# Attention's loads issued as pairs of half-size transfers, in a fused mLSTM, MoE and MLP kernel

## The chip, the cores and the metric

The kernel runs on one core of a Trainium2 chip. The metric is device time in microseconds (us): of the kernel before, three runs gave 765.03 (median), 762.16 and 768.67. One further execution was profiled; the rows below are all of that execution.

## The reference, cut to what matters

Three stages follow each other. The first is a gated linear attention with a running state (mLSTM) over 4 batches, 8 heads, 768 steps and head dimension 40:

```python
for t in range(S):
    m_new = np.maximum(f_gate[:, :, t] + m, i_gate[:, :, t])
    f_stab = np.exp(f_gate[:, :, t] + m - m_new)
    i_stab = np.exp(i_gate[:, :, t] - m_new)
    C = f_stab[:, :, None, None] * C + i_stab[:, :, None, None] * np.einsum('bhd,bhe->bhde', vt, kt)
    n = f_stab[:, :, None] * n + i_stab[:, :, None] * kt
    ...
    y[:, :, t] = o * h_tilde / denom
```

The second sends each of the 3072 tokens to one of 8 experts of 384 places each (a greedy assignment by sorted logits) and computes `relu(x @ w1[e]) @ w2[e]`, with 320, 1024 and 320 features. The third is a dense `elu(x @ w_in) @ w_out` with 320, 2048 and 320 features. Only attention's loads are touched by the change.

## The kernel before, in words

**Attention** takes the sequence in 12 chunks of 64 steps and the batches in 2 pairs, which makes 24 units; `Attention.run` works through one unit u in each turn of its loop. Partitions 0 to 63 of a tile belong to one batch of the pair, 64 to 127 to the other. A unit needs two loads from HBM:

- `qk`: `self.QK[u]`, a tile of 128 partitions x (2, 8, 64) f32, keys first and queries second. The first four units load all 128 partitions (512 KB), later ones the 80 that hold data (320 KB). There are four such tiles, used in turn.
- `vk`: `self.VK[u]`, 128 partitions x 968 f32 (values, keys by token and output gates; 484 KB). There are six buffers.

In a turn, TensorE does the scores of unit u+2 (`scores`, L302) mixed with the products of unit u+1's queries with the state (`recall`, L391), then `P` times values (`values`, L377) mixed with the state's update (`state`, L404), then transposes and router logits (L446, L460) and the decay matrix of unit u+2 (`decay`, L311 to L315), which ScalarE turns into `W` (L317). VectorE weighs the scores (L356), adds the states (L415) and finishes the unit's rows `x` (L424 to L429), which GpSimd scales (L430).

**Weight chunks.** Beside attention, the MLP's weights are brought in and converted, a chunk `cx` at a time: `pull` issues the load of a chunk at the end of a turn (through `fetch`, L914), and `win_pieces` converts it on ScalarE (`cg`, L926, and `cF`, L933), VectorE (L939, L942) and GpSimd. There are 15 chunks: eight of `w_in` in 128 partitions (512 KB), two of `w_in` that are already brought in as two loads of 64 partitions (`lo` and `up`, 256 KB each, rows of 1 KB), and five of `w_out` (448 KB). Three buffers hold them.

**Order.** All these loads, and the stores of the finished rows (`rows_out`, L439: two of 64 partitions, 80 KB each), are issued by SyncE, strictly in program order; a load that must wait holds up all that stand behind it. `tie` makes the load of `vk` for unit u+4 wait for an operation of VectorE in turn u (`seeded`, L367), and that of `qk` for unit u+5 for another (`summed`, L415). Each transfer that SyncE issues takes one of eight semaphores in turn (DMAHW0 to DMAHW7 in the order's rows) and waits until the transfer that had it before has landed: eight can be under way.

After attention comes the router, then `Mlp.run`, a planned sequence over eight rounds of one expert each and the dense MLP on the same rows.

Of the kernel before, what the change touches and what calls it, by code (L numbers as in the profile page):

```python
# [119 lines left out]
class Attention:  # L120
# [150 lines left out]
    def load_qk(self, u, other=None):  # L271
        self.QK[u] = self.QKb[u % 4]
        z = slice(0, 128) if u < 4 else slice(64 - D, 64 + D)
        self.tie(self.nc.sync.dma_start(self.QK[u][z], self.qk[u, z]), other)

    def load_vk(self, u, other=None):
        self.VK[u] = self.two.tile([128, 968], F32, name="vk", bufs=6)
        self.tie(self.nc.sync.dma_start(self.VK[u], self.vk[u]), other)

    def value(self, u, h, r):  # L280
        return self.VK[u][r:r + 64, h * 41:h * 41 + 64]
# [596 lines left out]
class Mlp:  # L878
# [76 lines left out]
    def win_pieces(self, stage):  # L955

        nc = self.nc
        A, G = nc.scalar, nc.gpsimd
        wide = self.win.dtype != F32
        n = 512  # L960
        al, lo, up = slice(0, 128), slice(0, 64), slice(64, 128)
        tiles = {}
        total = 10 + EARLY * 320 // 448
        self.piece = self.got = 0

        def whole():
            return stage.tile([128, n], F32, name="cF")

        def get(i):
            k, h = divmod(i, 4)  # L970
            cs = slice(h * n, h * n + n)
            tiles[i] = [stage.tile([128, n, 2], I32, name="cx", bufs=3) if wide else None, None, None if wide else whole()]
            if i >= 10:
                cs = slice((i - 10) * 448, (i - 10) * 448 + 448)
                tiles[i] = [t if t is None else t[:, :448] for t in tiles[i]]
                loads = [(al, self.src(self.wout, al, cs))]
            elif k < 2:
                loads = [(al, self.src(self.win, slice(k * 128, k * 128 + 128), cs))]
            else:
                w = self.src(self.win, slice(256, 320), slice(h * 1024, h * 1024 + 1024))  # L980
                w = w.rearrange("p (k e t) -> e p k t", k=4, e=2)
                loads = [(lo, w[0]), (up, w[1])]
            self.fetch(loads, wide, tiles[i])

        def pull():
            if self.got < min(total, self.piece + 2 + wide):
                get(self.got)
                self.got += 1

        self.pull = pull  # L990
        for i in range(total):
            self.piece = i
            while i not in tiles:
                yield
            k, h = divmod(i, 4)
            cs = slice((i - 10) * 448, (i - 10) * 448 + 448) if i >= 10 else slice(h * n, h * n + n)
            if wide:
                w = 448 if i >= 10 else n
                tiles[i][1:] = stage.tile([128, n], F32, name="cg")[:, :w], whole()[:, :w]
            F = tiles[i][2]  # L1000
            yield from self.conv(wide, tiles.pop(i), top=True)
            if i >= 10:
                A.activation(self.first[0][:, cs], F, AF.Copy)
                yield
                nc.vector.tensor_tensor(self.first[1][:, cs], F, self.first[0][:, cs], op=ALU.subtract)
            elif k < 2:
                A.activation(self.wih[:, k, cs], F, AF.Copy)
                yield
                G.tensor_tensor(self.wil[:, k, cs], F, self.wih[:, k, cs], op=ALU.subtract)
            else:  # L1010
                w = self.wis.rearrange("p (k e t) -> p k e t", e=2, t=128)[:, 4 * h:4 * h + 4]
                F = F.rearrange("p (k t) -> p k t", t=128)
                A.activation(w[lo, :, 0], F[lo], AF.Copy)
                yield
                A.activation(w[up, :, 1], F[up], AF.Copy)
                yield
                nc.vector.tensor_tensor(w[up, :, 0], F[lo], w[lo, :, 0], op=ALU.subtract)
                yield
                nc.vector.tensor_tensor(w[lo, :, 1], F[up], w[up, :, 1], op=ALU.subtract)
            yield  # L1020
# [588 lines left out]
```

## Time and profile before

| | |
|---|---|
| median of three runs | 765.03 us |
| profiled execution | 764.96 us |
| its span, first to last instruction | 763.2 us |
| what lies outside the span | 1.76 us |
| TensorE busy in the span | 92% |
| mean granted TensorE clock | 0.96 of full speed |
| all loads and stores of SyncE's queue (q1) | 35.12 MB, 15.3% of the 16 DMA engines' span |

The profile's busy times are sums over the whole program, in which stages with different limits follow each other; a change in attention is read from the stretch of attention alone (0 to some 150 us). "DMA share" is the busy share of the 16 DMA engines; it can be a little over 1, since packets overlap. "Issue" in a list of waits or in the chain is time in which an engine waited for nothing that the profile shows.

### The profile page before, as it was taken

How to read it: one execution, taken by the hardware profiler on the slowest of the kernel's cores; microseconds unless marked ns; L12 is line 12 of the kernel's file. 1: busy time of each engine (PE TensorE's matmuls, PEld its weight loads, DVE VectorE, ACT ScalarE, POOL GpSimd, SP SyncE). 2: the span in 40 equal slices, each digit the busy share in tenths (PEclk: the TensorE clock that was granted, in tenths of full speed). 3: DMA queues.
4: the chain of work that ended last, by engine and by line, in shares of the span. 5: the costliest groups of instructions: out<-in, count | busy, mean ns of one | idle time of the engine just before them, and what ended most of it. 6: DMA issues, size and time to landing. Idle time of an engine off the chain costs nothing.

```text
span 763.2 us, 17860 instructions
## 1 busy us (share of the span) xinstructions
PE 702.8 (92%) x7229; PEld 639.9 (84%) x7232; DVE 545.0 (71%) x1610; ACT 377.9 (50%) x804; POOL 185.1 (24%) x242
## 2 busy tenths in 40 slices
PE   7788888825999999999999999999999999999994
PEld 4556566613989999998999999999999999999994
DVE  7786988876888968975796698569768824841551
ACT  4654445424465725742782366257527734642542
POOL 5564744225311401310211120112032310001001
PEclk9898999955999999999999999999999999999998
DMA  8686968236101400500220230023013321100000
GB/s 303 184 267 188 257 211 246 56 97 205 38 1 49 148 9 9 170 18 10 94 85 27 84 95 2 27 84 96 1 61 107 95 79 34 35 1 27 1 1 26
DMA packets 22435, 67.29 MB, mean 88 GB/s; under 512 B 3536, under 2 KB 7632, under 8 KB 22352
## 3 DMA queue, kind: packets, MB, share of 16 engines
q1 hardware_dynamic: 14240, 35.12, 15.3%
q0 software_dynamic: 8064, 30.94, 12.4%
q8 instruction: 56, 0.92, 0.5%
q14 instruction: 27, 0.22, 0.1%
q10 hardware_dynamic: 48, 0.10, 0.0%
HBM read 58.28 MB, written 7.86 MB: 87 GB/s over the span
## 4 chain that ended last, share of the span: by engine, by line
PE 74%; issue 11%; DVE 9%; ACT 2%; POOL 1%; DMA 1%; POOLq 0%; DVEq 0%; ACTq 0%
PE ph L1184 31%; PE acc L1323 6%; PE acc L1327 6%; PE acc L1324 6%; PE acc L1291 3%; PE pO L377 3%; PE acc L1293 2%; PE acc L1292 2%; PE pR L391 2%; PE pX L460 2%; PE acc L1278 1%; PE pX L446 1%; PE acc L1280 1%; PE pS L302 1%; PE ph L1137 1%
## 5 line engine op out<-in xcount | busy, mean ns | idle before, releaser
L1237 DVE SCALAR_TENSOR_TENSOR e<-e,ph 128x384 f32<-128x384 f32 x128 | 70.4, 551 | 51.5 <-ACT e L1234 50.8
L1233 ACT ACTIVATE e<-ph 128x384 f32<-128x384 f32 x128 | 62.3, 487 | 80.7 <-PE ph L1184 75.8
L1184 PE MATMUL ph<-yh,wih 128*128 128x384 f32 x256 | 89.5, 349 | 0.7 <-DVE xl L1145 0.3
L1201 ACT ACTIVATE gh<-ph 128x384 fp32r<-128x384 f32 x64 | 31.4, 491 | 115.4 <-PE ph L1184 87.0
L1184 PE MATMUL ph<-yh,wil 128*128 128x384 f32 x256 | 86.6, 338 | 0.0
L1333 POOL DMA_INDIRECT out_dram<-ot,idx x24 | 24.0, 1001 | 219.1 <-ACT ot L1054 216.2
L1061 DVE TENSOR_TENSOR gl<-e,gh 128x384 fp32r<-128x384 f32 x128 | 71.1, 562 | 1.8 <-ACT gh L1054 0.4
L1234 ACT ACTIVATE e<-e 128x384 f32<-128x384 f32 x128 | 67.3, 526 | 4.2
L1323 PE MATMUL acc<-woh,gh 128*128 128x320 f32 x216 | 68.3, 316 | 0.0
L1208 DVE SCALAR_TENSOR_TENSOR gl<-ph,gh 128x384 fp32r<-128x384 f32 x64 | 35.3, 553 | 45.6 <-ACT gh L1201 45.5
L1327 PE MATMUL acc<-woh,gl 128*128 128x320 f32 x216 | 66.8, 309 | 0.5 <-DVE gl L1061 0.5
L1324 PE MATMUL acc<-wol,gh 128*128 128x320 f32 x216 | 66.7, 309 | 0.0
L1184 PE MATMUL ph<-yl,wih 128*128 128x384 f32 x256 | 66.5, 341 | 0.0
L1054 ACT ACTIVATE gh<-e 128x384 fp32r<-128x384 f32 x96 | 49.0, 514 | 11.5 <-DVE e L1237 11.2
L1327 PE MATMUL acc<-woa,gl 128*128 128x320 f32 x168 | 52.4, 312 | 0.8 <-DVE gl L1061 0.8
L1323 PE MATMUL acc<-woa,gh 128*128 128x320 f32 x168 | 53.1, 316 | 0.0
L1184 PEld LDWEIGHTS ph<-yh,wih 128*128 128x128 f32 x256 | 48.2, 188 | 4.7 <-ACT yh L1296 4.1
L1324 PE MATMUL acc<-wob,gh 128*128 128x320 f32 x168 | 51.9, 309 | 0.0
L1184 PEld LDWEIGHTS ph<-yh,wil 128*128 128x128 f32 x256 | 48.1, 188 | 0.0
L1184 PEld LDWEIGHTS ph<-yl,wih 128*128 128x128 f32 x256 | 46.2, 188 | 0.0
L1065 POOL DMA_INDIRECT stg<-in_w1a_dram,wi x16 | 15.8, 985 | 122.5 <-DVE wi L819 117.3
L1184 PE MATMUL ph<-yh,wis 128*128 128x384 f32 x128 | 44.8, 350 | 0.0
(282 smaller groups left out, 2039.0 us busy)
## 6 DMA issues: line engine op xcount, KB each, us to landing
vk<-in_vk_dram SPq DMA_DIRECT2D x24, 484.0 KB, 5.6
qk<-in_qk_dram SPq DMA_DIRECT2D x20, 320.0 KB, 4.8
cx<-in_win_dram SPq DMA_DIRECT2D x8, 512.0 KB, 4.5
xd<-x SPq DMA_DIRECT2D x48, 80.0 KB, 3.1
wx<-in_wout_dram SPq DMA_DIRECT2D x9, 320.0 KB, 3.0
cx<-in_wout_dram SPq DMA_DIRECT2D x5, 448.0 KB, 4.2
qk<-in_qk_dram SPq DMA_DIRECT2D x4, 512.0 KB, 6.4
cx<-in_win_dram SPq DMA_DIRECT2D x4, 256.0 KB, 6.7
```

Source lines behind the costliest of these rows:

```text
L1054: self.nc.scalar.activation(out, x, AF.Copy)
L1061: self.nc.vector.tensor_tensor(out, x, y, op=ALU.subtract)
L1184: PE.matmul(p, w, x, start=k == 0, stop=k == 7)
L1201: nc.scalar.activation(h, p, AF.Relu)
L1208: nc.vector.scalar_tensor_tensor(l, p, 0.0, h, op0=ALU.max, op1=ALU.subtract)
L1233: nc.scalar.activation(e, p, AF.Relu, scale=-1.0)
L1234: nc.scalar.activation(e, e, AF.Exp, scale=-1.0)
L1237: nc.vector.scalar_tensor_tensor(e, e, -1.0, p, op0=ALU.add, op1=ALU.max)
L1323: PE.matmul(p, h[:, c], wh, start=f == 0, stop=False)
L1324: PE.matmul(p, h[:, c], wl, start=False, stop=False)
L1327: PE.matmul(p, l[:, c], wh, start=False, stop=f == 15)
L1333: s = nc.gpsimd.indirect_dma_start(out=self.out, out_offset=bass.IndirectOffsetOnAxis(ap=idx[:, t:t + 1], axis=0), in_=o, in_offset=None)
```

## The change

Three groups of loads are each issued as two transfers of half the bytes, into the same tiles. `qk` is divided between keys and queries (each half still has all its partitions, with rows of 2 KB instead of 4 KB), `vk` and the `cx` chunks of 128 partitions into partitions 0 to 63 and 64 to 127. Both halves of a load are tied to the same operation. The two chunks that were already divided, the stores, and everything after attention stay as they are.

```diff
     def load_qk(self, u, other=None):
         self.QK[u] = self.QKb[u % 4]
         z = slice(0, 128) if u < 4 else slice(64 - D, 64 + D)
-        self.tie(self.nc.sync.dma_start(self.QK[u][z], self.qk[u, z]), other)
+        for k in range(2):
+            self.tie(self.nc.sync.dma_start(self.QK[u][z, k], self.qk[u, z, k]), other)
 
     def load_vk(self, u, other=None):
         self.VK[u] = self.two.tile([128, 968], F32, name="vk", bufs=6)
-        self.tie(self.nc.sync.dma_start(self.VK[u], self.vk[u]), other)
+        for r in (0, 64):
+            self.tie(self.nc.sync.dma_start(self.VK[u][r:r + 64], self.vk[u, r:r + 64]), other)
...
             if i >= 10:
                 cs = slice((i - 10) * 448, (i - 10) * 448 + 448)
                 tiles[i] = [t if t is None else t[:, :448] for t in tiles[i]]
-                loads = [(al, self.src(self.wout, al, cs))]
+                loads = [(p, self.src(self.wout, p, cs)) for p in (lo, up)]
             elif k < 2:
-                loads = [(al, self.src(self.win, slice(k * 128, k * 128 + 128), cs))]
+                loads = [(slice(r, r + 64), self.src(self.win, slice(k * 128 + r, k * 128 + r + 64), cs)) for r in (0, 64)]
```

The order of SyncE's queue in the middle of attention, before: one turn's loads and stores, and what each waits for (a row's first name is the tile written).

```order
L439 DMA xd<-x 64x320 [waits DMAHW5_49,Pool_49]
L439 DMA xd<-x 64x320 [waits DMAHW6_49]
L914 DMA cx<-in_win_dram 128x1024 [waits DMAHW7_49,Activation_49]
L278 DMA vk<-in_vk_dram 128x968 [waits DMAHW0_49,DVE_49]
L274 DMA qk_112<-in_qk_dram 80x1024 [waits DMAHW1_49,DVE_49]
```

The same place in the changed kernel (its lines after the edits lie one or two lower):

```order
L441 DMA xd<-x 64x320 [waits DMAHW1_49,Pool_49]
L441 DMA xd<-x 64x320 [waits DMAHW2_49]
L916 DMA cx<-in_win_dram 64x1024 [waits DMAHW3_49,Activation_49]
L916 DMA cx<-in_win_dram 64x1024 [waits DMAHW4_49]
L280 DMA vk<-in_vk_dram 64x968 [waits DMAHW5_49,DVE_49]
L280 DMA vk<-in_vk_dram 64x968 [waits DMAHW6_49]
L275 DMA qk_112<-in_qk_dram 80x512 [waits DMAHW7_49,DVE_49]
L275 DMA qk_112<-in_qk_dram 80x512 [waits DMAHW0_49,PE_49]
```

Nothing changes places; a turn issues eight transfers instead of five, so the eight semaphores come round within one turn. Before, the first load that had to wait for a semaphore was the small `wg` (L160), the eighth of SyncE's queue; now it is a half of unit 1's `vk`.

On ScalarE the first consumers of the loads, before:

```order
L351 ACTIVATE sg<-vk 128x320 [waits DMAHW4_49]
L317 ACTIVATE W<-pF 128x512 [waits PE_49] x2
L334 ACTIVATE De<-pR 128x16 [waits PE_49]
L335 ACTIVATE Dt<-pR 128x16
L351 ACTIVATE sg<-vk 128x320 [waits DMAHW5_49]
```

and in the changed kernel:

```order
L353 ACTIVATE sg<-vk 128x320 [waits DMAHW7_49,DMAHW6_49]
L319 ACTIVATE W<-pF 128x512 [waits PE_49] x2
L336 ACTIVATE De<-pR 128x16 [waits PE_49]
L337 ACTIVATE Dt<-pR 128x16
L353 ACTIVATE sg<-vk 128x320 [waits DMAHW1_49,DMAHW0_49]
```

The instructions of ScalarE, VectorE, GpSimd and TensorE keep their order; an instruction that reads a whole tile now waits for two landings.

## Rows read from the trace of the kernel before

**Rows 1.** Page, part 1: busy us (share of the span) and instructions of each engine.

```profile
PE 702.8 (92%) x7229; PEld 639.9 (84%) x7232; DVE 545.0 (71%) x1610; ACT 377.9 (50%) x804; POOL 185.1 (24%) x242
```

**Rows 2.** Page, part 4: the chain that ended last, by engine.

```profile
PE 74%; issue 11%; DVE 9%; ACT 2%; POOL 1%; DMA 1%; POOLq 0%; DVEq 0%; ACTq 0%
```

**Rows 3.** Windows by stage: busy us and instructions, granted clock, DMA share, GB/s.

```profile
core 0: us, PE busy (x) PEld busy (x) DVE busy (x) ACT busy (x) POOL busy (x), PEclk, DMA share, GB/s
5.00:13.00 8.00, 6.58 (x121) 4.39 (x120) 5.88 (x14) 4.06 (x11) 3.91 (x16) 1.00 1.01 396
25.00:75.00 50.00, 43.04 (x1193) 31.23 (x1187) 35.00 (x81) 25.48 (x52) 29.25 (x29) 0.88 0.77 229
131.00:150.00 19.00, 17.08 (x449) 13.43 (x441) 15.45 (x43) 8.94 (x21) 5.02 (x6) 1.00 0.29 79
190.00:763.00 573.00, 561.46 (x3670) 537.19 (x3669) 397.35 (x1218) 289.48 (x618) 90.75 (x113) 0.99 0.16 51
```

**Rows 4.** DMA, 25 to 131 us: queues (packets, MB, share), transfers, KB, us to landing.

```profile
q1 hardware_dynamic: 9891, 24.40, 78.4%
q8 instruction: 20, 0.33, 1.3%
...
vk<-in_vk_dram SPq DMA_DIRECT2D x17, 484.0 KB, 5.4
qk<-in_qk_dram SPq DMA_DIRECT2D x17, 320.0 KB, 4.7
cx<-in_win_dram SPq DMA_DIRECT2D x7, 512.0 KB, 4.5
xd<-x SPq DMA_DIRECT2D x36, 80.0 KB, 3.3
cx<-in_wout_dram SPq DMA_DIRECT2D x5, 448.0 KB, 4.2
cx<-in_win_dram SPq DMA_DIRECT2D x4, 256.0 KB, 6.7
```

**Rows 5.** DMA, 5 to 13 us: SyncE's queue.

```profile
q1 hardware_dynamic: 1027, 3.17, 101.2%
```

**Rows 6.** DMA, 82 to 88 us: SyncE's queue, and what was issued.

```profile
q1 hardware_dynamic: 976, 1.54, 101.6%
...
cx<-in_win_dram SPq DMA_DIRECT2D x2, 256.0 KB, 6.6
...
xd<-x SPq DMA_DIRECT2D x2, 80.0 KB, 6.2
```

**Rows 7.** Unit by unit: line L429, once a turn, first and last start.

```profile
L429 DVE SCALAR_TENSOR_TENSOR x<-sg,pO x24: 433/446/476, 15.7 to 149.8; 128x320 f32<-128x320 f32 x24
```

**Rows 8.** Timelines of SyncE and ScalarE: chunks issued; the last one's first reader.

```profile
27.73 0.58 SPq L914 DMA_DIRECT2D cx<-in_win_dram  x1
...
34.51 0.58 SPq L914 DMA_DIRECT2D cx<-in_win_dram  x1
...
40.19 0.70 SPq L914 DMA_DIRECT2D cx<-in_win_dram  x1
...
46.57 0.54 SPq L914 DMA_DIRECT2D cx<-in_win_dram  x1
...
52.37 0.54 SPq L914 DMA_DIRECT2D cx<-in_win_dram  x1
...
113.87 1.04 SPq L914 DMA_DIRECT2D cx<-in_wout_dram  x1
122.25 0.61 ACT L926 ACTIVATE cg<-cx 128x448 f32<-128x448 f32 x1
```

**Rows 9.** DMA, 2.1 to 2.2 us: the first unit's vk, issued at 2.14 us.

```profile
vk<-in_vk_dram SPq DMA_DIRECT2D x1, 484.0 KB, 6.1
```

**Rows 10.** Timeline of ScalarE: the first readers of that load and of the decays.

```profile
8.48 0.45 ACT L351 ACTIVATE sg<-vk 128x320 f32<-128x320 f32 x1
9.06 0.60 ACT L317 ACTIVATE W<-pF 128x512 f32<-128x512 f32 x1
```

**Rows 11.** SyncE's issue instructions by line, ns min/median/max; semaphore instructions of two readers.

```profile
L278 SPq DMA_DIRECT2D vk<-in_vk_dram x24: 327/380/1601, 2.1 to 131.4; - x24
L274 SPq DMA_DIRECT2D qk<-in_qk_dram x24: 327/334/860, 1.2 to 125.9; - x24
L914 SPq DMA_DIRECT2D cx<-in_win_dram x12: 334/597/885, 15.7 to 84.6; - x12
L351 ACTq EVENT_SEMAPHORE  x20: 17/28/925, 21.2 to 145.0; - x20
L377 PEldq EVENT_SEMAPHORE  x1: 51/51/51, 147.2 to 147.2; - x1
```

**Rows 12.** SyncE's longest waits in attention: who, for whom, us, times, longest.

```profile
SPq L439 <- POOL x L430: 39.5, 24, 4.0
SPq L274 <- DVE rd L425: 24.1, 15, 4.5
SPq L278 <- DVE pO L367: 17.9, 11, 5.2
```

**Rows 13.** TensorE's waits that nothing explains, 0 to 155 us.

```profile
PE pS L302 <- issue: 7.1, 7, 1.7
PE pC L404 <- issue: 3.8, 3, 1.9
PE pX L460 <- issue: 2.1, 2, 1.8
PE pO L377 <- issue: 1.8, 2, 1.0
PE pR L391 <- issue: 1.4, 1, 1.4
```

**Rows 14.** A window in which the granted clock had fallen.

```profile
61.00:66.00 5.00, 4.76 (x80) 3.34 (x79) 3.76 (x9) 2.08 (x4) 2.62 (x3) 0.51 0.49 146
```

## The prediction

> **What bounds the kernel now.** I read the profile from the whole to the part. TensorE is busy 92% of the span [rows 1], and three quarters of the chain of waits that ended last are TensorE's own work [rows 2]. The windows by stage then show where this change can act at all: from 190 us on the DMA engines are 16% busy and TensorE 561 of 573 us, and none of the edited loads is issued there [rows 3]. Attention is another place. From 25 to 75 us the DMA share is 0.77, and TensorE still has idle time [rows 3]. One turn of the loop takes (149.8 - 15.7) / 23 = 5.83 us [rows 7]. So attention is a chain of small steps in which loads run several turns ahead, over DMA engines that are three quarters full. A slower load costs nothing until it has eaten its lead; what it costs beyond that goes into the end of the program one to one, since the router waits for the last unit.
>
> Sums are made against the profiled execution, 764.96 us; the median of the three runs is 765.03, which is the same. About 1% (7.65 us) is what a measurement of this kernel can tell from no change.
>
> **The change, part by part.**
>
> *More transfers on SyncE.* 24 loads of vk, 24 of qk, 8 + 5 chunks: 61 more transfers. By the medians of their lines [rows 11] that is 24 x 0.38 + 24 x 0.33 + 13 x 0.60 = 25 us more of issuing, spread over the stage. SyncE waits 39.5 + 24.1 + 17.9 = 81.5 us there for results of attention [rows 12]; the extra issues lie in these waits. A second half reaches the queue some 0.4 us after the first, and the stores behind it are late by a similar time, which nobody waits for within the turn. Cost 0. Were that cover gone, all 25 us would delay loads, not engines, and again the lead would count.
>
> *More waits on readers.* A reader of a whole tile now has two landings to wait for. A semaphore instruction takes 17 to 28 ns on ScalarE and 51 ns on TensorE's loading side [rows 11]. One more a turn on each, partly beside other work: between 0 and 24 x 0.08 = 1.9 us; I take 0.5.
>
> *Eight semaphores now cover half as many bytes.* Eight halves are about 8 x 0.25 = 2 MB under way, at the 396 GB/s of the first loads [rows 3] some 5 us of work, so the DMA engines do not run dry. Cost 0.
>
> *Half the partitions.* This is the term that matters. The halves of qk keep their partitions. Those of vk and of the chunks go to 64 partitions only. The kernel has such transfers already: the row stores and two chunks in pieces of 256 KB. A piece of 256 KB lands after 6.7 us, a whole chunk of 512 KB after 4.5 [rows 4]. To price it, let a and b be the us of DMA time per MB of whole and of 64-partition transfers. From 25 to 131 us, SyncE's queue took 78.4% of 106 us = 83.1 us for 24.40 MB, of which 36 stores and 4 pieces are 4.0 MB [rows 4]: 20.4 a + 4.0 b = 83.1. From 82 to 88 us, 101.6% of 6 us = 6.10 us for 1.54 MB, of which two pieces and two stores are 0.69 [rows 6]: 0.85 a + 0.69 b = 6.10. Together a = 3.08 and b = 5.05, a ratio of 1.64. Both sorts of narrow transfer have rows of 1 to 1.25 KB, so the ratio holds an unknown share for short rows, which vk and the chunks (3.9 and 4 KB) won't pay. Lower end: it is all short rows, and halves cost a = 3.08. Upper end: whole loads cost only what the first stretch shows, 101.2% of 8 us for 3.17 MB = 2.56 [rows 5], and the rest of 82 to 88 us is charged to narrow ones, b = (6.10 - 0.85 x 2.56) / 0.69 = 5.70. I take 4.5, nearer to 5.05, because the pieces are the same kind of load in the same queue.
>
> After the change qk's 5.57 MB cost 5.57 x 3.08 = 17.2 us, the old narrow 4.0 MB 20.2, and the newly narrow 14.8 MB 14.8 x 4.5 = 66.6: 104 of 106 us, against 83 before. The stage's transfers just fit. In a turn with a chunk: 1.02 x 4.5 + 0.16 x 5.05 + 0.33 x 3.08 = 6.4 us, 0.6 more than a turn. Chunks are issued in five turns running, from 27.73 to 52.37 us [rows 8], so loads fall behind by 3 us there; a turn without one needs 1.8 less than it lasts. The shortest lead that I found is a chunk's: issued at 113.87 us, read at 122.25 [rows 8], landed after 4.2 [rows 4], so 4.2 us are in hand. What is late next, if that doesn't do, is line L926 on ScalarE, and behind it in order L933, the gates and W, which VectorE and then TensorE wait for. At 4.5 the lead holds on the whole: I take 1.0 us for single late chunks. The ends: 0, and at 5.70 (with 2.56 for qk) 14.3 + 18.8 x 5.70 = 121.5 us, 15.5 too many, less 4.2 = 11.3.
>
> [...]
>
> *The start.* The first unit's vk lands at 2.14 + 6.1 = 8.24 us [rows 9], its reader L351 starts at 8.48, and W behind it at 9.06 [rows 10]. The engines are full there [rows 5], so its 0.50 MB take 1.27 us; at the ratio 4.5 / 3.08 = 1.46 that is 0.6 more, landing at 8.8, reader at 9.06 to 9.5, W 0.45 later. That is on the chain. Ends 0 and, at a ratio of 2.23, 1.4. I take 0.5.
>
> Sum: 764.96 + 0.5 + 1.0 + 0.5 + 0 + 0 = **767.0 us**, 0.3% slower, which can't be told from no change.
>
> **The rivals.**
>
> *Late chunks become the bound (slower).* The stage and the lead together have room for 106 + 4.2 = 110.2 us of transfers, of which 17.2 + 20.2 = 37.4 are qk's and the old narrow ones. If a newly narrow MB costs more than (110.2 - 37.4) / 14.8 = 4.9 us, that is 1.6 times a whole one, loads fall behind without end, ScalarE stands at L926, and each turn lasts as long as its transfers. From 5.4 on the loss is over 1%. At the upper end it is 764.96 + 11.3 + 1.4 + 0.5 = 778 us. [...] For it: the 6.7 us of the narrow pieces. Against it: short rows explain a part of that, and the turns without a chunk make up for some.
>
> *Code arrives sooner (faster).* TensorE's waits for nothing visible in attention sum to 7.1 + 3.8 + 2.1 + 1.8 + 1.4 = 16.2 us in 15 waits [rows 13], and 20 fetches of 16 KB of instructions run over the same DMA engines from 25 to 131 us [rows 4]. If such a fetch must wait for a load's share on its engine to end, half as long a share halves the wait: 764.96 - 8.1 = 757 us. [...] Against it: with halves on 64 partitions a share of half the bytes takes 0.73 to 1.1 of the time, and the fetch's own time stays.
>
> *Nothing happens.* If narrow loads of long rows cost as whole ones, every edit is covered: 765.
>
> **How the numbers follow.** Forecast (the stage just fits) 0.56, 764 to 772; late chunks 0.28, 772 to 782; nothing 0.09, 764 to 766; code sooner 0.07, 755 to 762. The predicted time is 767. The range from 760 to 780 leaves out about half of the code rival and the far end of the late chunks, with what no case covers. Faster by over 1% (below 757.3) 0.05; slower by over 1% (above 772.6) 0.28, nearly all of it late chunks; within 1% 0.67.
>
> **What would show it.** Right: a DMA share near 0.95 to 1.0 from 25 to 131 us at the same bytes; vk and chunks landing 2 us or more later than before, qk little changed; turns of 5.8 to 6.0 us; W of the first unit near 9.5 us; all stages after attention the same length. Late chunks: ScalarE idle before the chunk's first reader (L926, in the changed kernel L928) with a DMA as releaser, and a longer turn in the runs of turns with chunks. Code sooner: fewer or shorter unexplained waits of TensorE at the same landings. Wrong altogether: a difference that arises after 190 us, or a share that stays at 0.78.

## The result and the profile after

The changed kernel takes 770.60 us (median of 20 runs, 764.33 to 774.51); the kernel before, beside it on the same chip, 765.89 (20 runs, 762.01 to 769.89). The ratio is 1.0051, with a 95% interval of 1.0029 to 1.0073: slower by 3.9 us, which is less than the 1% that was set as the bound of "no change", but not zero. The profiled execution took 772.55 us, 7.6 us more than that of before, so it shows more loss than the medians have. (Ratios here and below come from runs side by side, without those over 1.5% above the fastest of their kernel, and need not be the quotient of two medians.)

**Where it arises.** The unit's last step, once a turn (it was L429 [rows 7]; name, count, ns minimum/median/maximum, first and last start):

```profile
L431 DVE SCALAR_TENSOR_TENSOR x<-sg,pO x24: 434/447/475, 19.0 to 158.6; 128x320 f32<-128x320 f32 x24
```

The first x is 3.3 us late (15.7 before), the last 8.8 (149.8 before), and a turn lasts (158.6 - 19.0) / 23 = 6.07 us against 5.83: 5.5 us more are lost behind the first x. Behind the last x lie 770.8 - 158.6 = 612.2 us of the span, before 763.2 - 149.8 = 613.4. So all of it is made in attention, 3.3 us of it before the first unit is done.

**The start.** SyncE's timeline (start, us, line, tile; a count stands for transfers in a row):

```profile
1.21 1.88 SPq L275 DMA_DIRECT2D qk<-in_qk_dram  x4
3.13 2.46 SPq L280 DMA_DIRECT2D vk<-in_vk_dram  x4
5.64 3.52 SPq L275 DMA_DIRECT2D qk<-in_qk_dram  x4
```

ScalarE's timeline, the rows that answer to [rows 10]; in brackets the idle time before and what ended it:

```profile
10.50 0.47 ACT L353 ACTIVATE sg<-vk 128x320 f32<-128x320 f32 x1 [1.93 <-DMA vk<-in_vk_dram]
10.88 0.58 ACT L319 ACTIVATE W<-pF 128x512 f32<-128x512 f32 x1
```

The first unit's vk is issued 1.0 us later than before (3.13 against 2.14 us), since four halves of qk go ahead where two whole ones did, and its reader starts 2.0 us later (10.50 against 8.48); ScalarE now stands idle 1.93 us for it, and W behind it is 1.8 us late.

From there to the first x the delay grows to 3.3 us, and TensorE's clock has a part in it. Its timeline, the two blocks of scores that follow, before:

```profile
10.46 1.15 PE L302 MATMUL pS<-qk 64*64 64x64 f32 x32
11.87 1.15 PE L302 MATMUL pS<-qk 64*64 64x64 f32 x32 [0.25 <-issue]
```

and in the changed kernel:

```profile
12.27 1.66 PE L304 MATMUL pS<-qk 64*64 64x64 f32 x32
14.40 1.90 PE L304 MATMUL pS<-qk 64*64 64x64 f32 x32
```

The two blocks take 1.3 us more. From 13 to 16 us the granted clock is 0.50 here (the row stands in the last section), after TensorE stood still 2.5 us for W; in the kernel before it was 1.00 in the same stretch.

**The stage.** Windows by stage, columns as in [rows 3]:

```profile
5.00:13.00 8.00, 4.79 (x76) 2.94 (x76) 5.41 (x13) 4.06 (x11) 2.30 (x10) 0.98 1.01 250
25.00:75.00 50.00, 39.68 (x1147) 28.95 (x1150) 36.76 (x85) 27.45 (x54) 29.75 (x31) 0.93 0.88 218
131.00:150.00 19.00, 15.66 (x495) 11.46 (x486) 14.85 (x36) 7.83 (x17) 6.43 (x7) 1.00 0.60 150
190.00:763.00 573.00, 566.88 (x3688) 540.35 (x3687) 401.62 (x1227) 294.23 (x630) 95.46 (x118) 0.99 0.16 54
```

The DMA engines are full from 5 to 13 us, as they were, and move 250 GB/s instead of 396. From 25 to 75 us they are busier (0.88 against 0.77) and move less (218 against 229). What was not moved by then is moved later: 0.60 from 131 to 150 us, where it was 0.29. The transfers from 25 to 131 us, columns as in [rows 4]:

```profile
q1 hardware_dynamic: 11387, 23.13, 88.9%
...
vk<-in_vk_dram SPq DMA_DIRECT2D x35, 242.0 KB, 5.6
qk<-in_qk_dram SPq DMA_DIRECT2D x34, 160.0 KB, 5.3
cx<-in_win_dram SPq DMA_DIRECT2D x18, 256.0 KB, 4.9
```

By the medians a half of vk lands after 5.6 us, a whole one did after 5.4: half the bytes take as long. TensorE's waits that nothing explains, 0 to 160 us, columns as in [rows 13]:

```profile
PE pO L379 <- issue: 5.8, 4, 2.7
PE pC L406 <- issue: 5.7, 4, 2.1
PE pS L304 <- issue: 4.0, 4, 1.6
PE pF L317 <- issue: 1.9, 1, 1.9
PE pR L393 <- issue: 1.8, 3, 0.8
PE pO L363 <- issue: 1.4, 1, 1.4
PE pX L462 <- issue: 0.4, 1, 0.4
```

They sum to 21.0 us. Before there were 16.2 [rows 13] and this sixth row, 17.1 in all:

```profile
PE pF L313 <- issue: 0.9, 1, 0.9
```

**No late chunk.** A chunk that came late would show as ScalarE idle ahead of L928 with a DMA as releaser; no such row exists. The thirteenth chunk, the one whose lead was measured before [rows 8], was issued at 119.97 us (SyncE's timeline) and read 8.9 us later, 8.4 before:

```profile
119.97 1.20 SPq L916 DMA_DIRECT2D cx<-in_wout_dram  x2
```

and its first reader in ScalarE's:

```profile
128.86 0.60 ACT L928 ACTIVATE cg<-cx 128x448 f32<-128x448 f32 x1
```

### The profile page after: what moved, and what is told of

It reads as the page before. It is cut to its first block, busy times and chain, and to the rows that moved or that the text cites. A ratio compares the mean times of both kernels' runs of the same rounds, so it can differ in the third digit from the quotient of the medians.

```text
span 770.8 us, 18012 instructions
## 1 busy us (share of the span) xinstructions
PE 704.6 (91%) x7232; PEld 641.3 (83%) x7232; DVE 544.3 (71%) x1610; ACT 378.5 (49%) x804; POOL 184.1 (24%) x242
## 4 chain that ended last, share of the span: by engine, by line
PE 73%; issue 11%; DVE 6%; DMA 4%; ACT 2%; POOL 2%; SPq 1%; POOLq 0%; ACTq 0%; DVEq 0%
PE ph L1186 31%; PE acc L1325 6%; PE acc L1329 6%; PE acc L1326 6%; PE acc L1293 3%; PE acc L1295 2%; PE acc L1294 2%; PE pO L379 2%; PE pR L393 2%; PE pX L462 2%; PE acc L1280 1%; PE pS L304 1%; PE acc L1282 1%; PE pX L448 1%; DMA vk<-in_vk_dram 1%
## 5 line engine op out<-in xcount | busy, mean ns | idle before, releaser
L1186 PE MATMUL ph<-yh,wil 128*128 128x384 f32 x256 | 86.6, 338 | 0.0
L1067 POOL DMA_INDIRECT stg<-in_w1a_dram,wi x16 | 15.7, 982 | 122.5 <-DVE wi L821 117.3
```

The lines of the kernel that those rows point to most:

```text
L1186: PE.matmul(p, w, x, start=k == 0, stop=k == 7)
```

## The experiments

Four theories go through them, by the letters of the expectations. A: the start makes most of the loss. B: the number of transfers, each with its issue and its semaphore, makes it. C: halves on 64 partitions keep the DMA engines busier through the whole stage. D: two effects of opposite sign, narrow halves that cost and shorter rows that let TensorE's code arrive sooner. Medians are of 12 runs (6 for vk alone by partitions).

### The start undone

```diff
-        for k in range(2):
+        for k in (slice(0, 2),) if u < 4 else (0, 1):
...
-        for r in (0, 64):
-            self.tie(self.nc.sync.dma_start(self.VK[u][r:r + 64], self.vk[u, r:r + 64]), other)
+        for r in (slice(0, 128),) if u < 4 else (slice(0, 64), slice(64, 128)):
+            self.tie(self.nc.sync.dma_start(self.VK[u][r], self.vk[u, r]), other)
```

> The changed kernel, but qk and vk of units 0 to 3 are whole loads again; 53 of the 61 splits stay. Theory A (most of the loss is made at the start: the first unit's vk lands 2.2 us later, ScalarE's W stands behind its reader, and TensorE's clock falls): sg of unit 0 starts near 8.5 us, W near 9.1, unit 0's x at 15.7 to 16, and the time is 0 to 1.5 us above the kernel before, a ratio of 1.000 to 1.002. Theory B (the number of transfers, each with its issue and its semaphore, spread over the stage): 53/61 of the loss stays, 4 us, ratio 1.005. Theory C (64-partition halves keep the DMA engines busier through the whole stage and units fall behind there): the same 1.004 to 1.005, with a DMA share of 0.88 from 25 to 131 us as in the changed kernel, and x falling further behind from unit to unit.

766.51 us; ratio 1.0014, 0.9980 to 1.0048. Of the 0.51%, 0.14 is left where B and C had 0.4 to 0.5; the interval reaches up to them, so this alone does not decide. Its profiled execution was a long one (770.18 us). In it the start is regained but for 0.4 us at the first x, and 6.4 us are lost behind it, with a DMA share of 0.91 from 25 to 75 us: this one execution makes its loss in the stage. ScalarE's timeline, and then the x as above:

```profile
9.14 0.47 ACT L353 ACTIVATE sg<-vk 128x320 f32<-128x320 f32 x1 [0.57 <-DMA vk<-in_vk_dram]
```

```profile
L431 DVE SCALAR_TENSOR_TENSOR x<-sg,pO x24: 434/447/475, 16.1 to 156.6; 128x320 f32<-128x320 f32 x24
```

### The start alone

The same two conditions turned round (u >= 4 whole), put into the kernel before, chunks whole.

> The kernel before with qk and vk of units 0 to 3 alone split as in the change (keys and queries; partitions 0 to 63 and 64 to 127); all later loads and all chunks whole. Theory A (the start is the larger part): sg of unit 0 at 10.4 to 10.6 us, unit 0's x at 18.9 to 19.1, 3.2 to 3.4 us late, and the delay is kept to the last x; ratio 1.003 to 1.006, as the whole change (1.0051). If later turns win the delay back (loads then have a longer lead) or the loss is made in the stage: ratio 0.999 to 1.002, with the last x less than 1.5 us late.

769.64 us; ratio 1.0027, 0.9987 to 1.0067. Between the two expectations. The reader of vk started at 9.57 us, not at 10.50, although the loads of units 0 to 3 are those of the changed kernel, in the same order: the landing differs by 1 us between the two executions. The same two views:

```profile
9.57 0.47 ACT L353 ACTIVATE sg<-vk 128x320 f32<-128x320 f32 x1 [1.00 <-DMA vk<-in_vk_dram]
```

```profile
L431 DVE SCALAR_TENSOR_TENSOR x<-sg,pO x24: 434/446/476, 16.8 to 154.1; 128x320 f32<-128x320 f32 x24
```

The first x is 1.1 us late here and the last 4.3, so a delay at the start was not won back in this execution; why it grew with whole loads behind it is not shown. By the ratios the start alone is 0.27 of the 0.51%, and the rest without it 0.14. That leans towards A and does not show it: both intervals hold 1, and they overlap nearly whole.

### The first reader of vk moved behind W

```diff
-        self.opens(0)
         self.both(self.scores(0))
...
         self.decay(1)
+        self.opens(0)
         self.both(self.scores(1))
```

> The changed kernel with all its halves, but ScalarE does the first unit's output gates (sg, the first reader of vk) after the two first W instead of ahead of them. Theory A: vk lands as late as in the changed kernel (10.4 us), but W starts at 9.1 as before, the scores of unit 1 follow without the gap of 2.5 us, the granted clock does not fall at 12.7 us, and unit 0's x is at 15.7 to 16.5; the time is 0 to 2 us above the kernel before, ratio 1.000 to 1.0025. Theories B and C: the start makes little, ratio 1.004 to 1.005 as in the changed kernel.

768.44 us; ratio 1.0058, 1.0019 to 1.0096: no gain. W starts at 9.06 us as in the kernel before, and yet the first x comes at 19.0. ScalarE's timeline, TensorE's longest wait from 9 to 16 us, and the x:

```profile
9.06 0.60 ACT L319 ACTIVATE W<-pF 128x512 f32<-128x512 f32 x1 [0.48 <-PE pF L317]
```

```profile
PE pS L304 <- DMA qk<-in_qk_dram: 2.3, 1, 2.3
```

```profile
L431 DVE SCALAR_TENSOR_TENSOR x<-sg,pO x24: 434/446/478, 19.0 to 156.6; 128x320 f32<-128x320 f32 x24
```

A's chain (vk, sg, W) is not the whole of it. With W on time, the scores of unit 2 wait for that unit's qk, the third load of qk, which stands in SyncE's queue behind both of the first vk. In the changed kernel the wait for W covered this one. It is not one late load but the queue of the first loads that is late. TensorE runs slower for a time here too (a matmul of L313 takes 0.61 us at 17.93 us, 0.38 at 9.71; the mean granted clock from 13 to 25 us is 0.86, 0.94 in the kernel before): these scores start 2.4 us late, the x 3.3.

### By columns instead of by partitions

In the kernel before, qk as in the change, and:

```diff
-        self.tie(self.nc.sync.dma_start(self.VK[u], self.vk[u]), other)
+        for c in (slice(0, 484), slice(484, 968)):
+            self.tie(self.nc.sync.dma_start(self.VK[u][:, c], self.vk[u, :, c]), other)
...
             t = x[p].rearrange("p a b -> p (a b)") if wide else F[p]
+            if p == slice(0, 128):
+                n = src.shape[1] // 2
+                for c in (slice(0, n), slice(n, 2 * n)):
+                    self.nc.sync.dma_start(t[:, c], src[:, c])
+                continue
```

> Every load that the change splits is split here too, 61 transfers more, but vk and the chunks by columns, so that each half has all 128 partitions. Theory A or C, if the 64 partitions are the cause (at the start or in the stage): DMA share from 25 to 131 us back near 0.78 to 0.82; vk of unit 0 is issued 1.0 us later than in the kernel before, behind two more halves of qk, and lands 1.0 us later (reader at 9.5, not 10.5); the time is 1 to 2 us above before, ratio 1.001 to 1.003. Theory B (the number): reader of vk at 10.4, ratio 1.005 to 1.006, and packets on SyncE's queue up from 14240 to near twice that.

762.24 us (760.16 to 767.03); ratio 0.9953, 0.9920 to 0.9987. In attention there are as many transfers as in the change, each of as many bytes, and the time is below that of the kernel before. (The condition on `p` also halves the nine loads of `wx`, weights that SyncE issues behind attention's last loads; the edit of vk alone, below, is free of that.) B falls for these loads: 61 more issues and the second semaphores cost nothing here that shows. What is left between this kernel and the change in attention is the cut into 64 partitions. The first stretch (windows), the reader of the first vk (ScalarE's timeline) and the transfers from 25 to 131 us:

```profile
5.00:13.00 8.00, 5.97 (x120) 4.09 (x118) 5.88 (x14) 4.05 (x11) 3.83 (x16) 1.00 1.02 354
```

```profile
8.77 0.47 ACT L353 ACTIVATE sg<-vk 128x320 f32<-128x320 f32 x1 [0.20 <-DMA vk<-in_vk_dram]
```

```profile
q1 hardware_dynamic: 16309, 25.22, 79.1%
...
vk<-in_vk_dram SPq DMA_DIRECT2D x36, 242.0 KB, 4.7
```

354 GB/s against the change's 250; the reader 0.3 us later than before, not 2.0; a half of vk lands after 4.7 us. TensorE's unexplained waits, 0 to 160 us:

```profile
PE pC L406 <- issue: 4.9, 4, 1.5
PE pO L379 <- issue: 2.9, 3, 1.4
PE pS L304 <- issue: 1.4, 2, 1.0
PE pR L393 <- issue: 0.9, 2, 0.5
PE pX L462 <- issue: 0.9, 1, 0.9
```

11.0 us, 6.1 less than before. That the time fell was in no expectation.

### vk alone, by partitions and by columns

The edits of vk above, in the kernel before.

> The kernel before with vk alone issued as two halves of 64 partitions; qk and chunks whole. vk of unit 0 is issued at 2.14 us as before. Theory A with the 64 partitions as the start's cause: reader of vk near 9.5 to 9.7 (1.0 to 1.2 us late), unit 0's x 1 to 2.5 us late, ratio 1.001 to 1.004; the other 1.0 us of the changed kernel's delay is the earlier issue of qk's halves. Theory B: 24 of 61 transfers, so 24/61 x 4.7 = 1.8 us, ratio 1.002, evenly over the stage. Theory C: vk is 11.6 of the 14.8 newly narrow MB, so about 0.8 of what the stage loses.

> The kernel before with vk alone issued as two halves by columns, 128 partitions and rows of 1.9 KB each; it differs from vk in two halves of 64 partitions (774.9 us, ratio 1.013) in nothing but how the tile is cut. Theory D: no loss at the start (sg near 8.5 us), DMA share from 25 to 131 us 0.77 to 0.80 against 0.87 there, unexplained waits of TensorE 13 to 15 us, ratio 0.996 to 0.999. If the number of transfers were the cause: ratio 1.01 as with 64 partitions.

By partitions 774.86 us, ratio 1.0128, 1.0076 to 1.0180; by columns 764.23, ratio 0.9965, 0.9934 to 0.9995. The same tile, the same bytes, the same number of transfers: the cut alone differs, and the two intervals lie on either side of 1. By partitions, the first stretch and the first reader:

```profile
5.00:13.00 8.00, 4.07 (x56) 2.21 (x54) 5.24 (x13) 3.46 (x10) 1.74 (x4) 0.99 1.03 246
```

```profile
11.25 0.47 ACT L352 ACTIVATE sg<-vk 128x320 f32<-128x320 f32 x1 [2.67 <-DMA vk<-in_vk_dram]
```

and by columns:

```profile
5.00:13.00 8.00, 6.55 (x121) 4.32 (x119) 5.97 (x15) 4.12 (x11) 3.80 (x15) 1.00 1.01 369
```

```profile
8.76 0.47 ACT L352 ACTIVATE sg<-vk 128x320 f32<-128x320 f32 x1
```

369 / 246 = 1.50 is what the cut into 64 partitions cost over full engines at the start, with the same whole loads of qk beside it in both. From 25 to 131 us the SyncE queue's share is 86.6% by partitions and 81.3% by columns, and by columns 25.0 MB went through instead of 23.3. vk by partitions is also clearly slower than the whole change, which does the same to vk and more: the parts don't add.

### Chunks alone, and the change with qk whole

> The kernel before with the chunks alone in two halves of 64 partitions (5.9 of the 14.8 newly narrow MB, none of them in the first 15 us). Theory A (the loss is at the start): nothing, ratio 0.999 to 1.001. Theory C (narrow halves cost in the stage): DMA share from 25 to 75 us up from 0.77 to 0.82 to 0.86, loads behind by a few us there, ratio 1.001 to 1.005. The late chunk of the prediction: ScalarE idle ahead of L928 with a DMA as releaser.

767.81 us; ratio 1.0030, 0.9997 to 1.0063, which is not clear of no change. In the profiled execution, a short one (764.22 us), the DMA share is 0.80 from 25 to 75 us, there is no late chunk either, and the last x is 0.5 us late.

> The changed kernel with qk whole again: vk and chunks in halves of 64 partitions, 37 of the 61 splits. If effects add: by the parts alone (vk 1.013, chunks 1.003) ratio 1.012 to 1.018; by the change less the split of qk (1.0051 - 0.0085) 0.995 to 0.999; these can't both hold. If the parts share one cost (DMA time of 64-partition halves at the start and in the stage), as much as or more than the change, since qk's whole transfers ahead of vk push it back no less: sg of unit 0 at 10.5 to 11.2 us, unit 0's x 3.3 to 4 us late, ratio 1.005 to 1.013.

772.32 us; ratio 1.0078, 1.0048 to 1.0108: below the sum of the parts and above the change less qk. Reader of vk at 10.47 us, first x 3.4 us late, 271 GB/s from 5 to 13 us. Here vk is issued at 2.13 us, as in the kernel before, and its reader is as late as in the change. So neither the halves of qk nor the later issue make the change's start; the third of the expectations holds.

### vk and chunks by columns, qk whole

> vk and chunks in two halves by columns, qk whole. It is the kernel with all three by columns (762.2 us, ratio 0.9953) less the split of qk. If the split of qk costs 0.85% by itself, whatever stands beside it: ratio 0.985 to 0.990. If the effects don't add (what one split brings depends on what lies beside it in the queue): ratio 0.994 to 0.998 as with all three or with vk alone (0.9965). Theory D: unexplained waits of TensorE 11 to 14 us.

762.93 us; ratio 0.9962, 0.9930 to 0.9994: again faster than before, and like all three by columns. The start is that of the kernel before, with 394 GB/s (windows, ScalarE's timeline, the x):

```profile
5.00:13.00 8.00, 6.45 (x121) 4.40 (x120) 5.88 (x14) 4.06 (x11) 3.91 (x16) 1.00 1.04 394
```

```profile
8.47 0.45 ACT L352 ACTIVATE sg<-vk 128x320 f32<-128x320 f32 x1
```

```profile
L430 DVE SCALAR_TENSOR_TENSOR x<-sg,pO x24: 434/448/476, 15.7 to 145.1; 128x320 f32<-128x320 f32 x24
```

Unexplained waits of TensorE sum to 9.7 us, with vk alone by columns to 12.7.

### qk alone, three ways

> The kernel before with qk alone issued as two transfers (keys, queries), all partitions kept. Theory D (two effects of opposite sign: halves on 64 partitions cost DMA time, halves with shorter rows let TensorE's code arrive sooner): no narrow half here, so the start is not late (sg of unit 0 at 8.5 to 9.2 us) and unexplained waits of TensorE before 160 us fall from 17.1 us towards the 11.0 of the halves by columns, in proportion to the bytes about 1.5 us: ratio 0.997 to 0.999. Theory B (the number of transfers costs): 24 of 61, ratio 1.001 to 1.002.

770.93 us; ratio 1.0085, 1.0058 to 1.0113. Every theory missed it: no half is narrower than before, and the loss by the median is larger than that of the whole change.

```diff
-        self.QKb = [one.tile([128, 2, 8, 64], F32, name=f"qk{i}") for i in range(4)]
+        self.QKb = [one.tile([128, 2, 9, 64], F32, name=f"qk{i}") for i in range(4)]
...
-        self.tie(self.nc.sync.dma_start(self.QK[u][z], self.qk[u, z]), other)
+        self.tie(self.nc.sync.dma_start(self.QK[u][z, :, :8], self.qk[u, z]), other)
```

> The kernel before with one transfer for each qk as there, but into tiles with a gap of 256 bytes between keys and queries, so that each partition's row arrives in two pieces of 2 KB: as many packets on SyncE's queue as with qk alone in two transfers, and 24 transfers fewer. If the shorter piece is what matters (theory D), times and unexplained waits as with qk in two transfers: ratio 0.997 to 0.999. If it is the half as many bytes under a semaphore, or the number of transfers, no change: ratio 0.999 to 1.001.

764.70 us; ratio 0.9989, 0.9957 to 1.0022. Shorter pieces of qk neither cost nor bring anything; the unexplained waits are 20.8 us.

> The kernel with qk alone in two transfers once more. It was slower by 0.85% where theory D had 0.1 to 0.3% faster, but its profiled execution (766.6 us) was one of its shortest (766.0 to 773.3) and doesn't show where the 5 us lie. If the loss is real: median 769 to 772, ratio 1.005 to 1.011, and this profile shows it before 152 us, in a place where the kernel with qk in pieces of 2 KB in one transfer has nothing: a load or a store of a row behind the added transfers, or falls of TensorE's clock. If it was chance: ratio 0.998 to 1.003.

770.38 us; ratio 1.0046, 1.0010 to 1.0082. The loss is there again, and again the profiled execution is a short one (766.17 us). It shows a late start: vk, whole, is issued at 3.13 us behind four halves of qk, and its reader starts at 10.04 us, at 9.07 in the execution profiled first.

```profile
10.04 0.47 ACT L352 ACTIVATE sg<-vk 128x320 f32<-128x320 f32 x1 [1.47 <-DMA vk<-in_vk_dram]
```

```profile
L430 DVE SCALAR_TENSOR_TENSOR x<-sg,pO x24: 434/448/476, 17.0 to 153.2; 128x320 f32<-128x320 f32 x24
```

So 1.3 us of its delay is at the start and 2.1 more follow in attention; as a whole this execution is 1.2 us longer than that of the kernel before, so it does not show where the median's loss lies. Why it is the two transfers of qk, which cost nothing beside vk and chunks by columns, stays open.

## Why the prediction was right or wrong

It said 767.0 us, 0.3% slower; measured are 0.5%, within the range. The cause was named rightly, the halves on 64 partitions. That the sum came so near is in part luck: of its 2.0 us, 1.0 was for late chunks and 0.5 for second waits, which no run showed, while the start cost several times its 0.5, and the profiled executions lost time in the stage in a way that the sum did not have.

**The start: the step that failed.** Forecast 0.5 us, at most 1.4; measured 3.3 at the first x, and in the executions with vk by partitions 1.1, 3.3, 3.3, 3.4 and 4.0. The step priced one load, the first unit's vk, up to its first reader. It left out that the loads around it are slowed too, so that W was 1.8 us late where 0.5 was forecast; that the scores of unit 2 need qk's third load; and that TensorE ran slower there. In the changed kernel the granted clock was 0.50 from 13 to 16 us. In the other three executions whose first x is 3.3 us late or more TensorE was slower too: with vk alone by partitions a block of scores took 1.91 us and with qk whole 1.73, against 1.15 before (the mean granted clock from 13 to 25 us was 0.78 in both, 0.94 before); with the first reader moved it was the matmul of L313 behind the scores, 0.61 against 0.38. In the execution with 1.1 a block took 1.15. In the four TensorE had first stood still 2.3 to 3.2 us, for W or for qk; that the standstill brings the clock down is not shown. The sum ought to have gone along the queue: at 4.05 us per MB (101.2% of 8 us for the 2.00 MB that went through from 5 to 13 us) instead of the 2.56 of the kernel before. The engines are full there, before and after, so nothing is hidden; the trace said so [rows 5].

**SyncE's issues.** Cost 0, argued for the loop, and in the kernels by columns it holds; the loss with qk alone keeps it from being shown for every load. At the start vk is issued 1.0 us later. In the change that cost nothing, since with qk whole the reader was as late; by columns the reader was 0.3 us late, with qk alone 0.6 and 1.6.

**The price of narrow halves** was near. With the prediction's prices for the other transfers, from 25 to 131 us 88.9% of 106 us are 94.2; less 34 loads of qk (5.57 MB at 3.08, 17.2 us) and the old narrow ones (34 stores and 4 pieces, 3.83 MB at 5.05, 19.3), 57.7 us remain for 13.7 MB: 4.2 us per MB, where 4.5 was taken. Of short rows against partitions, the partitions are shown for vk: halved by columns, with rows half as long, the queue's share per MB is that of before (81.3% for 25.0 MB against 78.4% for 24.4).

As a ratio the prediction took 4.5 / 3.08 = 1.46. The runs gave 4.2 / 3.08 = 1.36 in the stage, and 1.50 at the start in the pair that differs in the cut of vk alone (369 GB/s by columns against 246 by partitions).

**The share of 0.95 to 1.0** did not come, it was 0.89. The sum held the bytes of 25 to 131 us fixed; with units late, loads are too, and 1.3 MB moved out of the window. The stage had room behind 131 us that the bound of 106 us left out.

**Late chunks (1.0 us, and as a rival 0.28)** were not seen in any run, and no reader of a vk or a chunk on ScalarE or VectorE, the first unit's aside, waited more than 0.6 us for a transfer. So the 5.5 us that the profiled execution lost after its first x are not late loads at readers. 3.9 us more of unexplained waits of TensorE are the only part of it that a view names, and these waits do not follow the time: they sum to 16.8 us with vk alone by partitions and to 13.8 with the first reader moved, below the 17.1 of the kernel before, and both are slower. How the stage loses its share stays open. The rival's range went 4 us beyond its own sum of 778 us; no run shows that part.

**Extra waits of readers (0.5).** By columns every reader has them, and the kernel is faster; no run shows the term.

**Signs.** Landings 2 us later: no, half a load lands about when the whole one did. W of unit 0 near 9.5: it was 10.9. Turns of 5.8 to 6.0: 6.07. Stages after attention the same: yes, within 1.2 us.

**Code arrives sooner (0.07)** is not what the change did, with 21.0 us of such waits against 17.1. In the three kernels by columns it is what the trace would show if it were so (11.0, 12.7 and 9.7 us, each kernel faster, each interval below 1). But shorter rows of qk alone left the waits at 20.8, and two executions of one program gave 13.0 and 18.8 (qk alone). That code arrives sooner is argued, not shown.

**Open**: how the stage loses behind the first unit; why qk in two transfers loses by itself; why the parts don't add; what the columns gain by. All three by columns, at 762.24 us, has the lowest ratio, 1% below the change (0.9953 / 1.0051); the other two by columns can't be told from it.

## What to carry to other kernels

If a load of 128 partitions has to be cut, don't cut it by partitions: halves of a tile by columns kept 354 to 394 GB/s over full engines, halves by partitions 246 to 285. A cut along the free dimension is no safe gain either: qk, cut so between keys and queries with all its partitions kept, lost 0.5 and 0.9% alone and nothing that shows beside vk and chunks by columns. Price a slower load at the start of a program along the whole queue, up to the last load that the first steps need, not at its own first reader; taking one reader out of the way bares the next. Add what a fall of TensorE's clock may cost behind such a delay: here 1.3 us in two blocks of scores, at a granted clock of 0.50. And measure parts beside the whole: the parts of this change, alone, lose 1.3 (vk), 0.5 to 0.9 (qk) and 0.3% (chunks, not clear of 0), and together 0.5.

## What the runs showed of the hardware that was not expected

- Halves by columns with rows of 1.8 to 2 KB ran slightly faster than whole loads with rows twice as long, in three kernels (ratios 0.9953, 0.9962, 0.9965); in the first two the loads of `wx` were halved as well.
- The landing of the first unit's vk differs by 1 us between executions with the same loads ahead of it: readers at 9.07 and 10.04 us in one program, at 9.57 and 10.50 in two with the same first transfers.
- TensorE's clock fell at the start of the changed kernel: a granted clock of 0.50 from 13 to 16 us, with TensorE busy all the while, after it had stood still 2.5 us for W.

```profile
13.00:16.00 3.00, 3.00 (x49) 2.45 (x47) 0.69 (x1) 0.00 (x0) 2.68 (x15) 0.50 1.11 301
```
